# A scan, eight routed experts and a Fourier mixer on one core: turned second layers, sorted last experts, 128-row blocks with stationary rows, and new orders

## The chip, the cores and the metric

The kernel runs on one core of a Trainium2 chip. The metric is the device time of one execution in microseconds. Three executions of the kernel before gave 446.72, 448.24 and 451.06 us; the median is 448.24.

## What is computed

Three networks follow one another: a chunked linear-attention scan, a mixture of eight experts in which the gate of a token can keep the expert of the token before, and a Fourier mixer with a two-layer network.

```python
# scan over a sequence of 768, for 4 batches and 8 heads
M = np.einsum('bhin,bhjn->bhij', Cc, Bc) * L          # L: decay between i and j, causal
y = M @ xc + (Cc @ state) * decay_to_i
state = decay_full * state + sum_j(Bc * xc * decay_from_j)
# experts: 3072 tokens of 256, 8 experts of 256 x 1024 x 256
e = fresh_e if s == 0 or local_gate < 0.5 else prev_e
out[b, s] = p[e] * (np.maximum(x[b, s] @ w1[e], 0.0) @ w2[e])
# mixer
u = x + np.real(np.fft.fft(np.fft.fft(x, axis=1), axis=2))
un = (u - mean) / sqrt(var + 1e-6)
return u + np.maximum(un @ w_ch1, 0.0) @ w_ch2
```

## The kernel before

Each value of the two-layer networks is split in a high and a low part, and a product is three matmuls: high by high, high by low, low by high. All instructions stand in an order that the program text fixes; each engine takes its own in that order, and SyncE (SP) takes the loads in order too.

*Scan* (`phase_a`). Twelve rounds (six chunks of 128 tokens, two pairs of batches) run `scores`, `mask`, `intra`, `keep`, `carry`, `rows`; `state_mm` multiplies the state's update. `routing` finds expert and rank of a chunk's tokens in small VectorE steps that a queue spreads over the rounds (`gap`, `place`), and `leave` scatters the rows, by the addresses `si`, into `xs_buf`, sorted by expert. When the last chunk but one has left, `xe`, the first 256 rows of expert 0, is loaded.

*Experts* (`ffn`, `moe_expert`). The first 256 rows of expert 0 (`EARLY`) go first, then its rest, then the seven others by size, with the capacities `CAPS`. In the first layer a 128 x 128 block of w1 is stationary and the expert's n rows move (`mm1`); ScalarE writes the relu `hh`, VectorE the low part `hl`. In the second layer a 128-row tile of `hh` or `hl` is stationary and 256 columns of w2 move, 24 matmuls for each tile, however many rows it has (`mm2`). `evac` scales a tile and GpSimd (POOL) scatters it into `y_tok` by token. Meanwhile the next expert's weights are loaded (`load_w`) and split (`high` on ScalarE, `low` on VectorE) and its rows transposed (`split_x`). `prep_wch` converts the mixer's weights in eight chunks. Behind the experts stands a branch on overfull experts (`overflow`, line 936), which isn't taken here.

*Mixer*. `load_z` and `load_k` read `y_tok` back by batch, `fold` reduces 768 points to six products of 128, `stage_a`, `correct` and `stage_b` are the transforms as matmuls, `residual` adds rows and mix, `center_` subtracts the mean. `group` runs the two-layer network for 512 rows at a time, six times; a batch has six tiles of 128 rows. `keep_clock` issues matmuls whose result isn't used, and so does `warm` in the scan.

Of the kernel before, what the change touches and what calls it, by code (L numbers as in the profile page):

```python
# [7 lines left out]
FP32 = mybir.dt.float32  # L8
# [12 lines left out]
CAPS = (128, 480, 448, 416, 416, 384, 352, 320)  # L21
# [5 lines left out]
CP, CT = 128, 129  # L27

# [8 lines left out]
WARM = 10  # L37
CA = {}
_o = 0
for _n, _w in (  # L40
    ("pm", 2), ("cmask", 128), ("w1", 9), ("ident", 128), ("w0", 9), ("tri", 128), ("ones", 128),
    ("tbl", 8), ("tid", 24), ("rid", 4), ("sel", 128), ("dlt", 12), ("cap", 8),
):
    CA[_n] = (_o, _w)
    _o += _w
# [5 lines left out]
def tile_kernel(ctx: ExitStack, tc: tile.TileContext, io):  # L51
# [9 lines left out]
    wst = ExitStack()  # L61
    wraw = wst.enter_context(tc.tile_pool(name="wraw", bufs=2))
    wsp = wst.enter_context(tc.tile_pool(name="wsp", bufs=2))
# [25 lines left out]
    y_tok = dram.tile([NTOK, D], FP32, name="y_tok")  # L89
    groups = set()  # L90
# [15 lines left out]
    def prep_wch(i, pool):  # L106
        n = 512
# [8 lines left out]
        else:  # L116
# [8 lines left out]
            dst = [t.rearrange("p k d -> p (k d)") for t in dst]  # L125
        hw, lw = raw[:, :, 1], raw[:, :, 0]
        v = pool.tile([128, n], I32, tag="cv", name="cv")
        e = pool.tile([128, n], I32, tag="ce_", name="ce_")
        r = pool.tile([128, n], FP32, tag="cr", name="cr")
# [6 lines left out]
        vf = v.bitcast(FP32)  # L136
        A.activation(out=dst[0], in_=vf, func=ACTF.Copy)
        ef = e.bitcast(FP32)
        G.tensor_tensor(out=ef, in0=vf, in1=dst[0], op=ALU.subtract)
        G.tensor_tensor(out=dst[1], in0=ef, in1=r, op=ALU.add)  # L140
# [5 lines left out]
    def expert(j):  # L146

        if j not in regs:
            regs[j] = nc.values_load(
                who[0:1, j:j + 1], engines=(mybir.EngineType.SP,), min_val=0, max_val=NE - 1 if j else EARLY,  # L150
                skip_runtime_bounds_check_because="a permutation of 1..7; a minimum with 256",
            )
        return regs[j]

    def load_w(e, part=None, static=False):

        i = bass.ds(e if static or e == 0 else expert(e), 1)
        if part != 1:
            r1 = wraw.tile([128, 2, F], FP32, tag="raw", name="r1")
            SP.dma_start(out=r1, in_=io["w1"][i].rearrange("o (k p) f -> p (o k) f", p=128))  # L160
            raws[e, 0] = r1
        if part != 0:
            r2 = wraw.tile([128, 8, D], FP32, tag="raw", name="r2")
            SP.dma_start(out=r2, in_=io["w2"][i].rearrange("o (k p) d -> p (o k) d", p=128))
            raws[e, 1] = r2

        def pieces():
            out = []
            for k, n, sh in ((0, "w1", [128, 2, F]), (1, "w2", [128, 8, D])):
                r = raws.pop((e, k))  # L170
                hi = wsp.tile(sh, FP32R, tag=n + "h", name=n + "h")
                lo = wsp.tile(sh, FP32R, tag=n + "l", name=n + "l")
# [16 lines left out]
                for q in range(2):  # L189
                    if not (ahead and k):  # L190
                        high(q)
                    if ahead:
# [13 lines left out]
    def keep_clock(pool, n):  # L206

        wps = pool.tile([128, 512], FP32, tag="mm1", name="wps")
        for _ in range(n):
            PE.matmul(out=wps, lhsT=fa[:, 0, :], rhs=fa[:, 0:4, :].rearrange("p n k -> p (n k)"), start=True, stop=True)  # L210
# [7 lines left out]
    def phase_a():  # L218
        with ExitStack() as st:
# [15 lines left out]
            def load(c, names=("ct", "bt", "x", "bn")):  # L235
# [8 lines left out]
            rp, dps = mb[:, 0:256], mb[:, 256:384].rearrange("p (u d) -> p u d", u=2)  # L244
# [3 lines left out]
                wsp.tile(sh, FP32R, tag=n, name="scr")  # L248
# [118 lines left out]
            st2 = [big.tile([128, 2, 64], FP32, name=f"st{q}") for q in range(2)]  # L367
# [84 lines left out]
            def state_mm(i):  # L452

                c, bp = pairs[i]
                for u in range(2):
                    for q in range(4):
# [966 lines left out]
```

## Time and profile before

| | |
|---|---|
| time of three executions | 446.72, 448.24, 451.06 us |
| the profiled execution | 449.59 us |
| its span, first to last instruction | 447.8 us |
| TensorE busy with matmuls | 420.5 us, 94% |
| VectorE, ScalarE, GpSimd busy | 270.1, 182.3, 147.6 us |
| mean granted TensorE clock | 0.981 |

The profile is of one execution. A matmul's end is modelled and matmuls overlap, so that a busy TensorE is not yet one at its peak, and busy time holds the matmuls that only keep the clock. The time is 1.8 us longer than the span. A granted clock of 1.00 is 2.4 GHz, 0.50 is 1.2 GHz.

### The profile page before, as it was taken

The page shows a single profiled execution, that of the slowest core. Times are in us where ns is not written, and L with a number is a line of the kernel's source. Part 1 is how long each engine was busy: PE and PEld are TensorE (multiplying, and loading weights), DVE is VectorE, ACT ScalarE, POOL GpSimd, SP SyncE. Part 2 cuts the span into 40 slices and gives each one's busy share as a digit, 9 for nine tenths or more (in the row PEclk, how much of TensorE's full clock was granted, in tenths as well). Part 3 has the DMA queues.
Part 4 walks back from the last instruction along what each step waited for, and adds up shares of the span by engine and source line. Part 5 has one row for each costly group of instructions (what it writes and reads, how often), then busy time and mean ns, then how long its engine had stood idle before and what let it go on. Part 6 is the DMA issues. An engine that isn't in the chain of part 4 may idle for free.

```text
span 447.8 us, 8833 instructions
## 1 busy us (share of the span) xinstructions
PE 420.5 (94%) x3403; PEld 366.3 (82%) x3403; DVE 270.1 (60%) x717; ACT 182.3 (41%) x399; POOL 147.6 (33%) x191
## 2 busy tenths in 40 slices
PE   8798788899999999999989979999999999999997
PEld 4476666479999999999989937679899998998986
DVE  3668889864583747566576408857537586654341
ACT  2255455334555454555454312343413433332230
POOL 1264876531006162433405530818003431400000
PEclk9899999999799999999999969999999999999999
DMA  8799711227356363736463037001402010010101
GB/s 287 228 309 310 284 50 52 73 84 264 111 183 209 117 213 126 247 99 211 153 199 109 34 101 250 23 2 47 143 25 94 1 35 14 14 35 11 38 1 47
DMA packets 32650, 54.10 MB, mean 121 GB/s; under 512 B 3161, under 2 KB 21882, under 8 KB 32601
## 3 DMA queue, kind: packets, MB, share of 16 engines
q1 hardware_dynamic: 29272, 45.73, 31.2%
q0 software_dynamic: 2816, 7.45, 4.8%
q8 instruction: 28, 0.46, 0.4%
q10 hardware_dynamic: 512, 0.28, 0.2%
q14 instruction: 22, 0.17, 0.1%
HBM read 41.50 MB, written 12.08 MB: 120 GB/s over the span
## 4 chain that ended last, share of the span: by engine, by line
PE 76%; DMA 8%; DVE 6%; ACT 5%; issue 2%; POOL 2%; SPq 0%; POOLq 0%; ACTq 0%; DVEq 0%
PE mm L857 30%; PE mm L844 26%; DMA y_tok<-y,ids 5%; PE tl L495 3%; PE tp L871 3%; PE g L411 2%; PE mb L259 2%; PE f L1125 2%; DMA xk<-y_tok,rix 2%; DVE mt L419 1%; PE yb L442 1%; DMA xn<-xs_buf 1%; ACT x1t L449 1%; PE cps L1139 1%; PE yb L431 1%
## 5 line engine op out<-in xcount | busy, mean ns | idle before, releaser
L849 DVE SCALAR_TENSOR_TENSOR hl<-mm,hh 128x512 fp32r<-128x512 f32 (+8 forms) x120 | 68.9, 589 | 49.8 <-ACT hh L848 49.6
L848 ACT ACTIVATE hh<-mm 128x512 fp32r<-128x512 f32 (+8 forms) x120 | 61.6, 518 | 78.7 <-PE mm L844 78.4
L909 POOL DMA_INDIRECT y_tok<-y,ids x26 | 32.5, 1249 | 94.6 <-ACT y L908 75.0
L857 PE MATMUL mm<-w2h,hh 128*128 128x256 f32 (+3 forms) x224 | 63.4, 283 | 0.0
L857 PE MATMUL mm<-w2l,hh 128*128 128x256 f32 (+3 forms) x224 | 62.6, 280 | 0.0
L857 PE MATMUL mm<-w2h,hl 128*128 128x256 f32 (+3 forms) x224 | 62.6, 279 | 0.0
L857 PE MATMUL mm<-c2h,hh 128*128 128x256 f32 x192 | 54.5, 284 | 0.0
L857 PE MATMUL mm<-c2l,hh 128*128 128x256 f32 x192 | 53.8, 280 | 0.0
L857 PE MATMUL mm<-c2h,hl 128*128 128x256 f32 x192 | 53.8, 280 | 0.0
L844 PE MATMUL mm<-xh,w1h 128*128 128x416 f32 (+7 forms) x144 | 48.2, 340 | 2.9 <-DVE hl L849 2.4
L844 PE MATMUL mm<-xh,w1l 128*128 128x416 f32 (+7 forms) x144 | 47.4, 334 | 0.0
L857 PEld LDWEIGHTS mm<-w2l,hh 128*128 128x128 f32 (+3 forms) x224 | 40.1, 179 | 0.1
L857 PEld LDWEIGHTS mm<-w2h,hh 128*128 128x128 f32 (+3 forms) x224 | 40.1, 179 | 0.1
L857 PEld LDWEIGHTS mm<-w2h,hl 128*128 128x128 f32 (+3 forms) x224 | 40.0, 179 | 0.1
L844 PE MATMUL mm<-xh,c1h 128*128 128x512 f32 x96 | 39.5, 411 | 0.6 <-ACT xh L873 0.6
L183 DVE TENSOR_TENSOR w2l<-r,w2h 128x1024 fp32r<-128x1024 f32 (+1 forms) x18 | 22.0, 1228 | 27.1 <-ACT w2h L180 27.1
L844 PE MATMUL mm<-xh,c1l 128*128 128x512 f32 x96 | 37.9, 395 | 0.0
L844 PE MATMUL mm<-xl,w1h 128*128 128x416 f32 (+7 forms) x144 | 36.7, 336 | 0.0
L857 PEld LDWEIGHTS mm<-c2l,hh 128*128 128x128 f32 x192 | 36.2, 188 | 0.1
L857 PEld LDWEIGHTS mm<-c2h,hh 128*128 128x128 f32 x192 | 36.1, 188 | 0.1
L857 PEld LDWEIGHTS mm<-c2h,hl 128*128 128x128 f32 x192 | 36.1, 188 | 0.0
L419 DVE TENSOR_TENSOR mt<-g,ca 128x512 f32<-128x512 f32 x48 | 31.3, 676 | 6.7 <-PE g L411 6.6
(329 smaller groups left out, 840.2 us busy)
## 6 DMA issues: line engine op xcount, KB each, us to landing
r<-in_w_dram SPq DMA_DIRECT2D x16, 1024.0 KB, 9.1
rawc<-in_wc_dram SPq DMA_DIRECT2D x8, 512.0 KB
out_dram<-o SPq DMA_DIRECT2D x24, 128.0 KB, 1.7
z<-y_tok SPq DMA_DIRECT2D x3, 768.0 KB
xs_buf<-scr SPq DMA_DIRECT2D x8, 265.0 KB, 8.5
xn<-xs_buf SPq DMA_DIRECT2D x4, 530.0 KB, 6.5
c1h<-in_x_dram SPq DMA_DIRECT2D x4, 512.0 KB, 5.2
xk<-y_tok SPq DMA_DIRECT2D x4, 512.0 KB, 3.7
```

What stands on the lines that cost most here:

```text
L183: V.tensor_tensor(out=l_[:, x:y], in0=r_[:, x:y], in1=h[:, x:y], op=ALU.subtract)
L259: PE.matmul(out=ps[:, 0:w], lhsT=wrm[:, 0:128], rhs=wrm[:, 0:w], start=True, stop=True)
L411: PE.matmul(out=gp[q][:, u].rearrange("p h i -> p (h i)"), lhsT=lds[c]["bt"][r:r + 32, 2 * bp + u, :], rhs=ch[r:r + 32, u].rearrange("p q ...
L419: V.tensor_tensor(out=m[:, :, 2 * q:2 * q + 2, :], in0=gp[q], in1=cc("cmask").unsqueeze(1).unsqueeze(1).to_broadcast([128, 2, 2, 128]), op ...
L495: PE.matmul(out=tl[:, 128 * g:128 * g + 137], lhsT=x1t[:, g, u, :], rhs=ca[:, o:o + 137], start=(g == 0), stop=(g == 1), skip_group_check= ...
L844: PE.matmul(out=ps[:, 0:n], lhsT=w[:, d, f * 128:(f + 1) * 128], rhs=x[:, d, 0:n], start=(k == 0), stop=(k == 5))
L848: A.activation(out=hf, in_=ps[:, 0:n], func=ACTF.Relu)
L849: V.scalar_tensor_tensor(out=hl[:, f, 0:n], in0=ps[:, 0:n], scalar=0.0, in1=hf, op0=ALU.max, op1=ALU.subtract)
L857: PE.matmul(out=ps[0:m, :], lhsT=h[:, f, t * 128:t * 128 + m], rhs=w[:, f, :], start=(k == 0), stop=(k == 23))
L871: PE.transpose(ps[d][:, t * 128:(t + 1) * 128], src(t, d), ident)
L909: w = G.indirect_dma_start(out=y_tok, out_offset=bass.IndirectOffsetOnAxis(ap=ids[0:m, t:t + 1], axis=0), in_=y[0:m, :], in_offset=None, b ...
L1125: PE.matmul(out=ps[:, k2, :], lhsT=r[:, zi, :], rhs=fa[:, ci, :], start=(i == 0), stop=(i == len(terms) - 1),)
```

## The change

It joins several edits.

- *Turned second layers.* For experts with n rows, n not a multiple of 128 and at most 480, the second layer has a 128 x 128 block of w2 stationary and n columns of `hh` or `hl` moving, twice 24 matmuls. The result is the transpose of what is wanted: ScalarE copies it (`yt`), and TensorE transposes it back under the next expert's first layer (`flush`).
- *Blocks of 128 rows.* Where n is 128, the rows are stationary and w1 moves, 512 columns at a time: 12 matmuls in place of 48. Eight transposes bring the relu back.
- *Sorted last experts.* `PLACE` sets a new order of sizes, with two experts of 416 rows last. Their rows are sorted by token into `xs_part` (`sort_rows`). Expert 6 then computes its first 288 rows, in which lie those of batches 0 and 1; expert 7 its first 128, with those of batch 0, and then its other 288; and at last expert 6 its other 128. Batch 0's transform is issued between these pieces (`rest`, `turn`), in tiles that free weight buffers lend (`homes`).
- *Orders.* At the scan's end `leave` and the addresses come ahead of the last chunk's steps; the last chunk's ranks in expert 0 begin behind row 256, so that its scatters don't wait for `xe`. Loads of weights in the scan stand behind a GpSimd `memset` (`held`). Rows are loaded two experts ahead. Batch 1's fold is all on VectorE; batches 2 and 3 have one correction together (`nyquist`). The branch on overflow comes at the end, and recomputes the mixer.
- *Scan.* `carry` and `state_mm` work on halves of the array in place of quarters.
- `keep_clock` is no longer called, and `warm` at the scan's end three times, not four.

```diff
-CAPS = (128, 480, 448, 416, 416, 384, 352, 320)
+CAPS = (128, 480, 448, 384, 352, 320, 416, 416)
+PLACE = (7, 6, 3, 2, 1, 5, 4)
+SORTED = (NE - 2, NE - 1)
+LEAD = {NE - 2: (2 * S, 288), NE - 1: (S, 128)}
...
@@ carry
-                        for q in range(4):
-                            r, o = 32 * q, 64 * (q % 2)
+                        for g in range(2):
+                            r = 64 * g
                             PE.matmul(
-                                out=yb[o:o + 64, q // 2, 128 * u:128 * u + 128], lhsT=s_st[bp][r:r + 32, u, :],
-                                rhs=ops[i][0][r:r + 32, u, :], start=(u == 0), stop=False, skip_group_check=True,
+                                out=yb[:, g, 128 * u:128 * u + 128], lhsT=s_st[bp][r:r + 64, u, :],
+                                rhs=ops[i][0][r:r + 64, u, :], start=(u == 0), stop=False, skip_group_check=True,
                             )
...
@@ the rounds of the scan
-                if i in (5, 7):
-                    ws = load_w(0, i // 7)
+                if i in (6, 8):
+                    g = load_w(0, i // 8, late=True)
+                    ws = g if i == 6 else ws
...
-                    leave(0)
-                    leave(0)
+                    gap(3, True)
+                    while scq:
+                        leave(0)
...
@@ ffn
+        flip = n % 128 and n <= 480
...
+        if n == 128:
+            for f in range(4):
+                hook(f)
...
+            for q in range(2):
+                ps = ps1.tile([128, CAP], FP32, tag="mm1", name="mm1")
+                for k, (w, x, d) in enumerate(terms):
+                    PE.matmul(
+                        out=ps, lhsT=x[:, d, 0:n], rhs=w[:, d, q * 512:q * 512 + 512], start=(k == 0), stop=(k == 5)
+                    )
...
+            flush()
+            for q in range(2):
+                ps = pst.tile([128, CAP], FP32, tag="tp", name="tp")
+                for f in range(4):
+                    PE.transpose(ps[:, 128 * f:128 * f + 128], hr[:, 4 * q + f, :], ident)
...
+        if flip:
+            yt = back_of(e)
+            yt = [yt[:, d, 0:n] for d in range(2)]
+            for d in range(2):
+                ps = ps2.tile([128, CAP], FP32, tag="mm2", name="mm2")
+                for k, (f, h, w) in enumerate(order2):
+                    PE.matmul(
+                        out=ps[:, 0:n], lhsT=w[:, f, 128 * d:128 * d + 128], rhs=h[:, f, 0:n], start=(k == 0),
+                        stop=(k == 23),
+                    )
+                    if k == 11:
+                        hook(8 + 2 * d)
+                A.activation(out=yt[d], in_=ps[:, 0:n], func=ACTF.Copy)
+                hook(9 + 2 * d)
...
@@ experts
+                at = AT.get(e, (2, 3, 4, 5, 8, 8))
+                for _ in range(at.count(i) if more else 0):
+                    next(ws, None)
...
+                if more and (e, i) == (e, MORE.get(e, 9)):
+                    next(ws, None)
+                    ws = load_w(e + 2) if e + 2 < NE else None
...
@@ transform
+        moe_expert(pools, last, *cur, lambda i: next(late) if i == 4 else None, n=n7)
+        homes_z()
+        load_z(0)
+        moe_expert(pools, last, *cur, rest, n=CAPS[last] - n7, t0=1)
+        wt.pop(last)
+        homes(1, wide(last))
+        moe_expert(pools, last - 1, *most, turn, n=CAPS[last - 1] - n6, t0=3)
...
+    with tc.manual_schedule():
+        lead, nr = experts()
+        transform(lead)
+    with tc.If(nr > 1):
+        overflow(pools, nr)
+        transform(None)
```

The order on VectorE near the scan's end, where the last chunk but one gets its addresses `si` and the last chunk starts its routing (`mx`, `kd`, `ls`), before and then after:

```order
L508 TENSOR_REDUCE mx<-scr 128x2
L512 TENSOR_SCALAR kd<-scr 128x2
L515 TENSOR_TENSOR ls<-scr,mx 128x16
L521 SCALAR_TENSOR_TENSOR cand<-ls,cb 128x16
L524 TENSOR_REDUCE ff<-cand 128x2
L526 SCALAR_TENSOR_TENSOR kd<-kd,ff 128x2
L183 TENSOR_TENSOR w1l<-r_696,w1h 128x512
L603 TENSOR_REDUCE rk<-ro 128x4
L607 SCALAR_TENSOR_TENSOR si<-f__1270,rk 128x4
```

```order
L639 SCALAR_TENSOR_TENSOR si<-f__1197,rk 128x4
L660 TENSOR_SCALAR nfirst<-mb 128x1
L539 TENSOR_REDUCE mx<-scr 128x2
L543 TENSOR_SCALAR kd<-scr 128x2
L546 TENSOR_TENSOR ls<-scr,mx 128x16
L552 SCALAR_TENSOR_TENSOR cand<-ls,cb 128x16
L555 TENSOR_REDUCE ff<-cand 128x2
L557 SCALAR_TENSOR_TENSOR kd<-kd,ff 128x2
L212 TENSOR_TENSOR w1l<-r_767,w1h 128x512
```

The addresses stood behind seven instructions of the next chunk, and now stand ahead of them.

The order on TensorE around batch 0's transform (`f`: the second product, `cps`: the correction, `mix`: the second stage), before and then after:

```order
L1125 MATMUL f<-fa,r_5440 128x128 x6
L1139 MATMUL cps<-w,fa 128x1 x6
L1155 MATMUL mix<-fb,pt 128x129
L1156 MATMUL mix<-fb,pt 128x128
...
L1155 MATMUL mix<-fb,pt 128x129
L1156 MATMUL mix<-fb,pt 128x128
L210 MATMUL wps<-fa 128x512 x5
L871 MATMUL tp<-ca,n 128x128 x8
L844 MATMUL mm_5609<-xh,c1h 128x512
```

```order
L1451 MATMUL mix<-fb,pt 128x129
L1452 MATMUL mix<-fb,home 128x128
L965 MATMUL tp<-ca,yt 128x128 x4
L965 MATMUL tp<-ca,yt 32x128 x2
L910 MATMUL mm_3417<-w1h,xh 128x512
L910 MATMUL mm_3417<-w1l,xh 128x512
...
L910 MATMUL mm_3425<-w1h,xl 128x512 x2
L922 MATMUL tp<-ca,hr 128x128 x8
```

Between the mix and the first matmuls of the mixer's network (`c1h`) stood clock keeping; now expert 7's transposes back (`yt`) and expert 6's last block stand there, and the transposes of `n` come in the middle of that block's second layer.

The order on TensorE in expert 0's rest, 128 rows, first layer, before (one of eight column blocks) and then after (one of two):

```order
L844 MATMUL mm_1707<-xh,w1h 128x128
L844 MATMUL mm_1707<-xh,w1l 128x128
L844 MATMUL mm_1707<-xh,w1h 128x128
L844 MATMUL mm_1707<-xh,w1l 128x128
L844 MATMUL mm_1707<-xl,w1h 128x128 x2
```

```order
L910 MATMUL mm_1647<-w1h,xh 128x512
L910 MATMUL mm_1647<-w1l,xh 128x512
L910 MATMUL mm_1647<-w1h,xh 128x512
L910 MATMUL mm_1647<-w1l,xh 128x512
L910 MATMUL mm_1647<-w1h,xl 128x512 x2
L922 MATMUL tp<-ca,hr 128x128 x8
```

The operands have changed sides: the weights moved past are 512 columns wide, and the relu's eight transposes follow.

## Rows read from the trace of the kernel before

**Rows 1.** Table of stages: span, each engine's busy us (instructions), granted clock, DMA.

```profile
93.30:118.40 25.10, 24.20 (x178) 23.96 (x179) 13.49 (x43) 10.55 (x26) 5.06 (x6) 0.86 0.54 186
118.40:258.00 139.60, 136.82 (x980) 131.71 (x979) 86.45 (x136) 71.56 (x126) 52.22 (x41) 1.00 0.47 154
258.00:286.20 28.20, 23.77 (x93) 13.90 (x92) 16.23 (x57) 7.67 (x19) 9.14 (x17) 0.88 0.42 139
```

**Rows 2.** Chain that ended last, experts: start us, us, engine, tile, line.

```profile
105.33 1.30 PE mm L844 x12
...
118.61 10.40 PE mm L844 x48
129.01 0.88 PE tp L871 x8
129.88 11.28 PE mm L857 x96
...
184.18 9.24 PE mm L844 x48
```

**Rows 3.** The table of stages, two microseconds in expert 0.

```profile
110.00:112.00 2.00, 2.00 (x12) 2.00 (x11) 1.35 (x2) 0.28 (x2) 0.00 (x0) 0.50 0.04 12
```

**Rows 4.** Timeline between experts and mixer, by engine: idle before in brackets.

```profile
258.84 0.91 POOL L909 DMA_INDIRECT y_tok<-y,ids  x1 [0.59 <-ACT y L908]
...
264.49 1.43 SPq L1040 DMA_DIRECT2D z<-y_tok  x3
...
267.88 0.56 DVE L1070 TENSOR_TENSOR eo<-z 128x384 f32<-128x384 f32 x1 [14.79 <-DMA z<-y_tok]
...
261.07 11.75 PE L210 MATMUL wps<-fa 128*128 128x512 f32 x20 [3.06 <-ACTq L936]
...
274.96 1.79 PE L1125 MATMUL f<-fa,r 128*128 128x128 f32 x12 [0.79 <-DVE r L1086]
...
279.74 4.46 PE L210 MATMUL wps<-fa 128*128 128x512 f32 x10
284.03 1.15 PE L871 MATMUL tp<-ca,n 128*128 128x128 f32 x8
```

**Rows 5.** Timeline at the scan's end, by engine.

```profile
79.60 0.16 DVE L508 TENSOR_REDUCE mx<-scr 128x2 f32<-128x16 f32 x1
...
81.31 0.16 DVE L607 SCALAR_TENSOR_TENSOR si<-f__1270,rk 128x4 int32<-128x4 f32 x1
...
88.88 0.38 SPq L620 DMA_DIRECT2D xe<-xs_buf  x1
...
92.35 0.60 PE L871 MATMUL tp<-ca,xe 128*128 128x128 f32 x4
```

**Rows 6.** Timeline, SP and ScalarE: issue and first use of expert 7's w1.

```profile
218.96 0.37 SPq L160 DMA_DIRECT2D r<-in_w_dram  x1
...
224.88 1.06 ACT L180 ACTIVATE w1h<-r 128x1024 fp32r<-128x1024 f32 x1
```

**Rows 7.** The table of DMA issues: KB each, median us from issue to landing.

```profile
r<-in_w_dram SPq DMA_DIRECT2D x16, 1024.0 KB, 9.1
...
y_tok<-y,ids POOLq DMA_INDIRECT x26, 3.2
```

**Rows 8.** Chain that ended last, mixer's network.

```profile
316.84 11.19 PE mm L844 x48
...
379.04 1.23 PE cps L1139 x12
```

**Rows 9.** Instructions of the branch, line 936: ns, first start us.

```profile
L936 PEldq COMPARE_BRANCH  x1: 3662/3662/3662, 255.8 to 255.8; - x1
```

**Rows 10.** Timeline and chain of one round of the scan, TensorE.

```profile
52.63 0.41 PE L457 MATMUL mb<-xt,c2l 128*32 128x64 f32 x16
53.66 0.73 PE L495 MATMUL tl<-ca,x1t 128*128 128x137 f32 x4 [0.62 <-ACT x1t L449]
...
47.75 0.60 PE yb L431 x16
```

More of the change, by code (lines that the diff above doesn't have):

```diff
@@ L35 @@
 GATE = -1.5 * 2.0 ** -23
-WARM = 10
 CA = {}
@@ L582, in routing @@
                 )
+                if c + 2 == NC:
+                    PE.matmul(out=rp[:, 8:9], lhsT=cc("ones"), rhs=ac[:, 0:1, nb], start=True, stop=True)
                 exo = sm.tile([128, nb, NE], FP32, tag="exo", name="exo")
@@ L861, in ffn @@
+        for t in range(0 if flip else tiles):
+            ps = ps2.tile([128, CAP], FP32, tag="mm2", name="mm2")[:, 0:D]
+            m = min(128, n - 128 * t)
+            for k, (f, h, w) in enumerate(order2):
+                PE.matmul(
+                    out=ps[0:m, :], lhsT=h[:, f, t * 128:t * 128 + m], rhs=w[:, f, :], start=(k == 0), stop=(k == 23)
+                )
+                if n == 128 and k == 11:
+                    hook(12)
             evac(t, ps[0:m, :], m)
             hook(8 + t)
+    turns = [0]
@@ new lines, in transform @@
+        if lead is None:
+            homes_z()
+            for i in range(1, 3):
+                homes(i, wide(i))
+            for b in range(NB):
+                load_z(b)
+                load_k(b)
+                all_of(b)
+                for g in {1: (0, 1, 2), 3: (3, 4, 5)}.get(b, ()):
+                    group(g, lambda i: None, split_n(g))
+            return
+        most, cur, late = lead
+        last = NE - 1
+        n6, n7 = (LEAD[e][1] for e in SORTED)
+        nxt = None
@@ new lines, in rest @@
+        def rest(i):
+            if i == 0:
+                next(late)
+            if i == 10:
+                stage_a(0, 0)
+            if i == 7:
+                near = xp.tile([128, 4, D], FP32, tag=f"xl{NE % 2}", name="near", bufs=1)
+                two = sm.tile([128, 2 * D], I32, tag="cv", name="near").bitcast(FP32)
+                home["pt0"] = sm.tile([128, 4 * 128], I32, tag="cv", name="pt").bitcast(FP32)
+                home["pt0"] = home["pt0"].rearrange("p (a b) -> p a b", a=4)
+                home["near"] = near, [two[:, D * k:D * k + D] for k in range(2)]
+                load_k(0)
+                run(0, 0, 3)
+                run(0, 1, 3)
@@ new lines, in transform, with hook @@
+        for g in range(6):
+            cur = nxt
+            def hook(i):
+                nonlocal nxt
+                if (g, i) in ((1, 3), (1, 4), (1, 5)):
+                    next(nyq)
+                if (g, i) in ((0, 3), (1, 1), (2, 1)):
+                    load_k(g + 1)
+                if (g, i) == (0, 7):
+                    center(0, 4, 6, (A,))
+                if i == 10 and g < 5:
+                    nxt = split_n(g + 1)
+                for p in plan.get((g, i), ()):
+                    run(*p)
+                if (g, i) == (0, 7):
+                    scale(0)
+            group(g, hook, cur)
```

752 lines of the change are left out of this document (486 added, 266 removed), and 6 rows, old and new, of the table plan.

## Prediction

> **What bounds the kernel now.** Read first the table of stages [rows 1]: from 118.4 us on TensorE has a matmul in flight for 136.8 of 139.6 us, so there only fewer or cheaper matmuls help. Two stretches are different. From 93.3 to 118.4 us its clock averages 0.86, and from 258.0 to 286.2 us, between the last expert's last matmul and the first matmul of the last network, it is busy for 23.8 of 28.2 us, but with what? The timeline there [rows 4] answers: 20 rows of clock-keeping matmuls, and a chain of other units. The last scatter of expert rows starts at 258.84, the load of z that waits for it at 264.49, VectorE begins on z at 267.88 after an idle of 14.79 us, TensorE starts the second part of the first transform at 274.96 and transposes the result at 284.03. The 28.2 us are one latency chain, during which nothing of the experts is left to compute. So I ask of each part of the change whether it cuts matmul time, or puts work under that chain.
>
> **Prices of a matmul.** First layer: 48 matmuls take 10.40 us at 480 columns, 9.24 at 416 [rows 2] and 11.19 at 512 [rows 8], that is 217, 192.5 and 233 ns each, or 0.423 ns a column plus 16.6 ns. Second layer before: 96 of 256 columns in 11.28 us, 117.5 ns each [rows 2]. A turned one has n columns; with the same slope from that anchor it costs 212 ns at 480, 199 at 448, 158 at 352, 145 at 320 and 131 at 288. A 128-column matmul takes 108 ns (1.30 us for 12), a transpose 110 ns (0.88 us for 8) [rows 2].
>
> **The change part by part.**
>
> *Scan.* The carry goes from 8 matmuls on quarters of the array to 4 on halves, the state's product likewise with twice the columns. Today the carry takes 0.60 us for 16 passes of 128 columns, and the rows product 0.73 us for 4 passes of 137 on the whole array [rows 10]: 0.29 ns a column on a quarter, 1.33 on the whole. Half way, some 0.55, the carry costs 8 x 128 x 0.55 = 0.56 us, a gain of 0.04 a pair. The state's product goes from 0.41 us to about 0.56, but TensorE then stands idle for 0.62 us for the copy x1t anyway [rows 10], so that covers it; uncovered it is +0.15 x 10 = 1.5 us. I take 0, bounds -1 to +2 (the products are also twice as wide on VectorE and GpSimd). The Trainium skill, TensorE: Matmul & The Clock Gate, Part 3 (packing small matmuls), speaks against this edit: concurrency comes from many small tiles in distinct row and column groups. By that rule the carry gains nothing and the state's product doubles; the trace's cheap quarter passes agree with it, and the sum would be +2 instead of 0.
>
> *Scan's end.* The experts begin when xe lands: load at 88.88, transposes at 92.35 [rows 5]. That load waits for scatters whose addresses si come at 81.31, behind seven VectorE instructions of the next chunk that start at 79.60. The order in the section on the change shows si moved ahead of them, to about 80.0: **-1.3 us**, and the four scatters and the load follow. The warm-up matmuls that vanish stood in TensorE's wait for xe; removing them gains nothing. The last chunk's scatters no longer wait for xe, which only helps later loads.
>
> *Expert 0.* From 105.33 to the 480-row expert at 118.61 are 13.3 us [rows 2]. In it TensorE falls to the lower of its two levels, 1.2 GHz: granted 0.50 at 110 to 112 us [rows 3], after a run of 128-column matmuls; the average of 0.86 over 25.1 us [rows 1] makes that 7 us at half speed, so 3.5 us lost. Now: 12 matmuls of 512 columns 2.80, 8 transposes back 0.88, 8 for the next expert 0.88, second layer 24 x 117.5 ns = 2.82, and 0.6 us waiting for the relu between: 8.0 us. **-5.3 us**, if the clock holds; at 1.2 GHz for the last 5 us it is -2.8.
>
> *Experts 1 to 7, matmuls.* Second layers turned: 480 10.2, 448 9.5, 352 7.6 and 320 6.9 us, instead of 11.28, 11.28, 8.46 and 8.46: -5.3. The two 416s become 288 turned (6.3) and 128 (2.8) instead of 11.28: -2.2 each, -4.4. Turned outputs must be transposed back, 40 times 0.11: +4.4. First layers of the split ones: 288 columns 6.6 and a block of 128 rows 2.8 + 0.9 instead of 9.24: +1.1 each, +2.2. More transposes of inputs +0.4, waits for the relu in two blocks +1.2. Sum -1.5. The same stretch has 2.8 us without a matmul now; the turned outputs add two ScalarE copies an expert, and VectorE (86 of 139.6 us busy, [rows 1]) stays below TensorE. Giving 1.5 us for that, the stretch comes to **0**; bounds -2.5 and +4. The sorting adds some 30 small VectorE instructions and 8 scatters to engines with room, and its loads are issued two experts ahead.
>
> *Between experts and the last network*, now 28.2 us. Batch 0's rows are complete after the lead of expert 7. From there: copy and start of the scatter 0.8 us; start of scatter to load issue 5.65 us today [rows 4] (the median landing of a scatter is 3.2 [rows 7], so 3.7 to 5.7); load issue to VectorE's start 3.4; VectorE to the second product 7.1 (267.88 to 274.96): 15 to 17 us. TensorE has under it the rest of expert 7 (6.6 + 6.3) and the first product (1.5): 14.4, leaving a wait of 0.5 to 2.6; I take 1.5. From the second product to the transposes the chain is 9.07 us; TensorE has second product, correction and mix (274.96 to 279.74, 4.7), expert 7's transposes back (0.7), expert 6's block (2.8, 0.9, 0.6 of wait, half of 2.8): 11 us, so no wait. The block's other half covers the split of the transposed rows. What stays of the 28.2 us: both products, correction and mix 1.5 + 4.7 = 6.2, transposes 0.9, wait 1.5, 0.2 of slack = 8.8. **-19.4 us.** The clock keeping goes, and so does TensorE's 3.06 us of idle at the branch [rows 4].
>
> *Group 0 of the last network*: 30.6 us now (286.2 to 316.84 [rows 8]). Batch 1's second fold moves from GpSimd to VectorE (two parts took VectorE 6.8 us for batch 0, so +3.4), and batch 1's z is loaded only after expert 7's last scatters, which stand behind five row additions on GpSimd: by the delays above some 6 us after the group's start, where VectorE waits in order ahead of the subtractions that free TensorE's buffers. Its matmuls sum to 11.19 + 11.28 + 0.88 + 6.2 = 29.6, so 1.0 us of waits is in it now. I take 1.7 of waits for 1.0: **+0.7**, bounds -1 and +3.
>
> *Nyquist column.* One correction for two batches: **-1.2 us** (12 rows in 1.23 us [rows 8]); its small operations lie on GpSimd under group 1.
>
> *The branch* on the overflow moves to the end. TensorE's compare took 3.66 us [rows 9]. On SyncE it now follows the last output store, whose landing covers part of it: **+1.5**, bounds 0 and 3.7. The Trainium skill, Runtime: NRT & Kernel Launch, section on instruction fetch mechanics, says that a taken branch out of the current code window has its target fetched before execution goes on; the 3.66 us agree, and by it alone the term is +3.7.
>
> **Sum:** -1.3 - 5.3 + 0 - 19.4 + 0.7 - 1.2 + 1.5 = -25.0. From the profiled 449.59 us (span 447.8) this gives 424.6. That execution lies 1.35 above the median, so against the median of 448.24 I predict **423 us**.
>
> **Rivals.** (1) *Weights come late.* A load of 1 MB of w1 is issued at 218.96 and used at 224.88 without more wait [rows 6], so 5.9 us suffice there; the one landing that the page shows is 9.1 us [rows 7]. The stages of 320 and 288 rows leave, from the conversion that frees the buffer half way through a second layer to the use after three first-layer groups, only some 5.4 us. ScalarE would then wait in order and hold up the relus. For five experts, 1.6 us each that the three buffers don't absorb: +8, 431 us. Against it: before, the first conversion came after two groups, sooner than now.
> (2) *The cover tears.* If z of batch 0 waits for more than the one scatter (the load waits for every scatter in the queue, and chunks of weight conversion stand on GpSimd before it), each us over 17 is a TensorE wait, and after 3 us of idle the clock falls as behind 258.0: the average of 0.88 over 28.2 us [rows 1] is 6.8 us at half speed, 3.4 us lost. With 6.6 us of wait: +10, 433 us.
> (3) *Slower than before.* Late weights as in (1), but at the 9.1 us of the page: 3.7 us a load for seven experts, and each such idle also lowers the clock as it does behind 258.0, 3.4 us: 7 x 7.1 = 50, 473 us. It decides from 3.6 us lost per expert (25 / 7). Today's 5.9 us without wait speaks against it.
> (4) *The cover works better*: landing in 3.7 us, no stall in group 0, no cost of the branch: -7, 416 us.
>
> **How the numbers follow.** Forecast 0.5, (4) 0.2, (1) 0.14, (2) 0.1, (3) 0.03, the remaining 0.03 no effect because several terms cancel. The forecast's own terms leave 415 to 431; with (4) below and (1) and (2) above, the range is 411 to 435. A run of this kernel shows no difference below about 1%. Faster by over 1%: 0.94; within: 0.03; slower: 0.03.
>
> **What would show it.** Right: 12 matmuls of 512 columns for expert 0 at granted clock 1.00 and the 480-row expert starting near 112 us; between the end of the first layer of expert 7's rest and group 0's first matmul no TensorE gap above 3 us; group 0 starting near 259 us; the span ending 2 to 4 us after the last output store. Wrong: ScalarE's conversions of w1 waiting for a DMA, a clock below 1.00 behind expert 7, VectorE waiting for z under group 0's first layer for more than 4 us.

## The result, and the profile after

| | before | after |
|---|---|---|
| times | 446.72 to 451.06 us | 425.28, 421.84, 420.60, 420.29 us |
| median | 449.61 us (four runs) | 421.22 us |
| profiled execution, span | 449.59, 447.8 us | 425.28, 423.2 us |
| TensorE busy with matmuls | 420.5 us | 404.0 us |

The ratio is 0.940, with a 95% interval of 0.933 to 0.947: 27 us off. The profiled execution is the longest of those shown. A fifth, timed beside them, took 423.16 us. In the five, the time falls as the mean granted clock rises: 425.28 (0.980), 423.16 (0.984), 421.84 (0.992), 420.60 (0.996), 420.29 (0.998).

First the page of the kernel after, busy times and then the granted clock in 40 slices.

```profile
span 423.2 us, 8212 instructions
...
PE 404.0 (95%) x3063; PEld 353.6 (84%) x3063; DVE 281.3 (66%) x772; ACT 188.5 (45%) x411; POOL 144.9 (34%) x204
...
PEclk9899999868999999999999999999999999999999
```

The table of stages of the same execution, columns as in [rows 1]: the scan's end, expert 0's first 256 rows, its 128-row rest, experts 1 to 7 with batch 0's transform, and groups 0 and 3.

```profile
80.00:92.40 12.40, 11.45 (x65) 6.59 (x65) 8.30 (x46) 3.93 (x13) 4.97 (x7) 0.59 0.27 87
...
95.70:108.90 13.20, 13.18 (x99) 13.18 (x99) 6.67 (x28) 4.13 (x12) 2.94 (x3) 0.87 0.55 182
108.90:117.10 8.20, 7.83 (x55) 6.76 (x54) 4.96 (x9) 6.97 (x11) 0.98 (x1) 1.00 0.57 198
117.10:263.70 146.60, 144.74 (x936) 135.67 (x935) 109.63 (x241) 82.61 (x161) 55.71 (x57) 1.00 0.55 176
263.70:293.50 29.80, 29.63 (x207) 26.90 (x205) 21.43 (x66) 10.61 (x25) 7.43 (x13) 1.00 0.39 125
...
345.60:373.10 27.50, 27.50 (x195) 25.54 (x194) 18.93 (x63) 11.21 (x27) 6.98 (x16) 1.00 0.07 21
```

Experts 1 to 7 and the transform, which took 139.6 + 28.2 us in two stages [rows 1], are one stage of 146.6 us at full clock, and TensorE stands idle for 1.9 us of it. Group 0 begins at 263.7 us. Behind the first 20 us the clock falls only at the scan's end, to 1.2 GHz from 82 to 92 us and again around 97 us. In the kernel before the same table reads 1.00 from 76 to 100 us.

How the gap closed stands in the chain that ended last, after:

```profile
236.12 6.32 PE mm L932 x48
242.44 4.81 PE mm L950 x36
247.26 1.34 PE f L1393 x12
248.59 1.59 PE mm L950 x12
250.19 1.66 PE f L1393 x12
251.84 1.23 PE cps L1434 x12
...
260.81 0.60 DVE hl L926
261.45 0.99 PE tp L993 x7
```

The first product of batch 0 (`f`) runs inside expert 7's second layer, the second right behind it; between the correction and the transposes (`tp`) TensorE has expert 6's block, and it waits for nothing longer than 0.25 us.

### The profile page after: what moved, and what is told of

Read it like the earlier page. It is cut to its first block, busy times and chain, and to the rows that moved or that the text cites. A ratio compares the mean times of both kernels' runs of the same rounds, so it can differ in the third digit from the quotient of the medians.

```text
span 423.2 us, 8212 instructions
## 1 busy us (share of the span) xinstructions
PE 404.0 (95%) x3063; PEld 353.6 (84%) x3063; DVE 281.3 (66%) x772; ACT 188.5 (45%) x411; POOL 144.9 (34%) x204
## 4 chain that ended last, share of the span: by engine, by line
PE 79%; DVE 10%; ACT 5%; DMA 2%; issue 2%; POOL 0%; DVEq 0%; ACTq 0%
PE mm L932 27%; PE mm L974 18%; PE mm L950 11%; PE tl L524 3%; PE tp L993 3%; PE f L1393 2%; PE g L440 2%; PE mb L288 2%; DVE mt L448 2%; PE yb L471 1%; PE g L288 1%; PE mm L910 1%; DMA r<-in_w_dram 1%; ACT x1t L478 1%; DVE hl L939 1%
## 5 line engine op out<-in xcount | busy, mean ns | idle before, releaser
L939 DVE SCALAR_TENSOR_TENSOR hl<-mm,hh 128x512 fp32r<-128x512 f32 (+7 forms) x112 | 65.9, 593 | 46.2 <-ACT hh L938 45.8
L938 ACT ACTIVATE hh<-mm 128x512 fp32r<-128x512 f32 (+7 forms) x112 | 57.3, 521 | 67.3 <-PE mm L932 67.3
L932 PE MATMUL mm<-xh,w1h 128*128 128x288 f32 (+6 forms) x128 | 42.7, 340 | 1.5 <-DVE hl L939 1.0
L932 PE MATMUL mm<-xh,w1l 128*128 128x288 f32 (+6 forms) x128 | 41.3, 329 | 0.0
L950 PE MATMUL mm<-hh,w2h 128*128 128x288 f32 (+4 forms) x96 | 32.2, 335 | 0.0
L950 PE MATMUL mm<-hh,w2l 128*128 128x288 f32 (+4 forms) x96 | 31.6, 329 | 0.0
L932 PE MATMUL mm<-xl,w1h 128*128 128x288 f32 (+6 forms) x128 | 31.5, 328 | 0.0
L950 PE MATMUL mm<-hl,w2h 128*128 128x288 f32 (+4 forms) x96 | 31.5, 328 | 0.0
L932 PE MATMUL mm<-xl,c1h 128*128 128x512 f32 x96 | 29.9, 392 | 0.0
L932 PEld LDWEIGHTS mm<-xh,w1h 128*128 128x128 f32 x128 | 24.7, 193 | 4.2 <-DVE hl L939 2.6
```

The lines of the kernel that those rows point to most:

```text
L932: PE.matmul(out=ps[:, 0:n], lhsT=w[:, d, f * 128:(f + 1) * 128], rhs=x[:, d, 0:n], start=(k == 0), stop=(k == 5))
L938: A.activation(out=hf, in_=ps[:, 0:n], func=ACTF.Relu)
L939: V.scalar_tensor_tensor(out=hl[:, f, 0:n], in0=ps[:, 0:n], scalar=0.0, in1=hf, op0=ALU.max, op1=ALU.subtract)
L950: PE.matmul(out=ps[:, 0:n], lhsT=w[:, f, 128 * d:128 * d + 128], rhs=h[:, f, 0:n], start=(k == 0), stop=(k == 23),)
```

## The experiments

All were timed beside the kernel before, five rounds each but for e6 and e7 with three. The kernel before had medians of 446.55, 448.38 and 448.35 us beside e1 to e4, e5 to e8 and e9 to e12, so that ratios are compared; 0.01 is 4.5 us. The experiments overlap (e3's last block stands under the transform that e6 takes away), so that their effects don't add up to the 27 us. Not undone by themselves are the new places of the scatters and addresses, `held`, the loads two experts ahead and batch 1's fold.

| run | change to the kernel after | median, us | ratio, 95% interval |
|---|---|---|---|
| e1 | none | 420.51 | 0.941, 0.937 to 0.945 |
| e2 | second layers not turned | 423.89 | 0.950, 0.945 to 0.955 |
| e3 | 128-row blocks, w1 stationary | 438.54 | 0.981, 0.977 to 0.985 |
| e4 | scan on quarters | 422.32 | 0.946, 0.941 to 0.950 |
| e5 | no branch | 419.85 | 0.936, 0.931 to 0.940 |
| e6 | transform behind both experts | 443.94 | 0.990, 0.986 to 0.993 |
| e7 | block not under the transform | 429.42 | 0.957, 0.952 to 0.962 |
| e8 | count first | 420.62 | 0.939, 0.933 to 0.945 |
| e9 | e8, loads sooner | 419.93 | 0.938, 0.935 to 0.941 |
| e10 | e9, scan on quarters | 419.68 | 0.939, 0.935 to 0.943 |
| e11 | e10, three more matmuls | 417.75 | 0.933, 0.930 to 0.936 |
| e12 | a correction for each batch | 421.43 | 0.942, 0.937 to 0.946 |

**The same kernel (e1).** 

> The changed kernel once more, unchanged, as the base for the others. Theory A (the profiled execution was an unlucky one: its granted clock lay at 0.50 from 82 to 92 us and from 96 to 99 us, which the shorter times beside it did not have): the median comes to 420 to 422 us, and a profile with a mean granted clock of 0.99 or more has xe's transposes (line 993) start near 92 us instead of 94.68 and the span end near 418.5. Theory B (the late start of the experts is there in every execution): xe's transposes start at 94 us or later at full clock too.

The median bears out A's range, but the profile can't decide: it is again of the longest execution (424.63 us, clock 0.978), with the same fall at 82 to 92 us. The other six executions had a mean clock of 0.995 or 0.996. Half speed from 82 to 92 us alone costs 0.012 of such a mean, so they hardly had that fall. What a scan without it does can be read in e6 below, whose scan is that of the kernel after and whose clock held until the transposes of `xe`. In its timeline and its table of stages:

```profile
75.13 0.73 PE L524 MATMUL tl<-ca,x1t 128*128 128x137 f32 x4 [0.47 <-ACT x1t L478]
...
86.89 0.38 SPq L654 DMA_DIRECT2D xe<-xs_buf  x1
...
90.22 0.66 PE L993 MATMUL tp<-ca,xe 128*128 128x128 f32 x4 [1.21 <-DVE cnt L844]
```

```profile
80.00:90.30 10.30, 7.18 (x35) 3.85 (x35) 8.14 (x43) 3.45 (x12) 6.06 (x7) 1.00 0.24 79
```

The transposes start at 90.22 us, and B falls. The stretch from the scan's 21st rows product (`tl`) to them was 16.7 us before. With the scan of after it is 15.1 us at full clock (e6), 16.6 and 16.7 where the clock averages 0.72 from 80 to 92.4 us (e2, e7), and 17.8 where it averages 0.59 to 0.61 (after, e1, e3, e5, e12). So at full clock the change shortens it by 1.6 us, and the fall of the clock takes up to 2.7.

**Second layers not turned (e2).**

```diff
-        flip = n % 128 and n <= 480
+        flip = False
```

> The changed kernel with the turned second layers undone: every second layer multiplies 128-row tiles by 256 columns again, also those of the sorted experts' 288 rows. Theory A (turned layers are a small gain, since the transposes back eat most of it): 480 rows 11.3 for 11.4 us, 448 11.3 for 10.7, 352 8.5 for 8.3, 320 8.5 for 7.8, and 288 rows twice 8.5 for 7.1, so +4 us in all, 425 us. Theory B (nothing, since the second layers' time lies under loads and conversions of the next weights, which set the pace of the experts): within 1 us. Theory C (turned layers also shorten the chain to the scatter of batch 0, because their copies come late): below the base by 1 us or more.

0.009 of ratio, 4.1 us: A, though the intervals just touch. The chain of e2, 480 and 448 rows:

```profile
124.97 5.66 PE mm L974 x48
...
130.98 5.73 PE mm L974 x48
...
147.27 8.40 PE mm L974 x72
...
156.02 2.88 PE mm L974 x24
```

And the kernel after:

```profile
128.52 5.28 PE mm L950 x24
134.13 5.38 PE mm L950 x24
...
151.01 7.36 PE mm L950 x36
158.71 2.55 PE mm L950 x12
```

For 480 rows turning saves 11.39 - 10.66 = 0.7 us, and the eight transposes back take 0.9 (0.44 us for four in the same chain): nothing is gained. For 448 it is 11.28 - 9.91 = 1.4 us, for 0.9 us of transposes. By these rows the gain is larger where the last 128-row tile is not full; 480 fills most of it.

**The 128-row blocks with w1 stationary again (e3).** The branch `n == 128` of the first layer gives way to the loop over eight column blocks.

> The changed kernel with the three blocks of 128 rows (expert 0's rest, expert 7's first rows, expert 6's last) back to w1 stationary: 48 matmuls of 128 columns instead of 12 of 512 and eight transposes back. Theory A (what the blocks give is the clock: 128-column runs let TensorE fall to 1.2 GHz, as at 110 to 117 us of the kernel before): the granted clock reads 0.50 for some 7 us in at least expert 0's rest, +3 us for each block that falls, 424 to 431 us. Theory B (the clock holds, the cost is that of the matmuls alone): 48 x 71 ns = 3.4 us against 2.8 + 1.3 us with the transposes, so each block is 0.5 to 0.7 us shorter, 419 us.

17.9 us, more than either theory had. The table of stages of e3 over the three blocks: expert 0's rest, expert 7's first rows, expert 6's last.

```profile
108.90:122.50 13.60, 12.46 (x82) 12.32 (x81) 6.53 (x16) 7.30 (x15) 0.98 (x1) 0.75 0.34 110
232.60:241.50 8.90, 8.90 (x80) 8.71 (x79) 4.42 (x13) 4.24 (x13) 5.41 (x5) 1.00 0.21 76
261.00:279.30 18.30, 14.15 (x84) 14.01 (x82) 8.92 (x32) 4.41 (x14) 6.22 (x12) 0.72 0.19 59
```

With the rows stationary the first takes 8.2 us (table above), and the other two, after:

```profile
227.90:236.00 8.10, 7.67 (x53) 6.60 (x52) 5.00 (x10) 4.69 (x10) 5.19 (x5) 1.00 0.23 85
255.40:263.70 8.30, 7.99 (x55) 6.87 (x53) 7.94 (x26) 4.60 (x10) 6.20 (x12) 1.00 0.10 35
```

So 5.4, 0.8 and 10.0 us, 16.2 in all. In the middle block the clock holds, and 48 matmuls of 128 columns cost 112 ns each on average, not B's 71 (the chain has 1.29, 1.29 and 2.81 us for 12, 12 and 24; the prediction's own price was 108): 5.4 us, against 2.8 + 1.3. In the other two the clock falls, as A says, but not by the 128 columns alone, since the middle block holds 1.00 with the same 48. In both TensorE had stood idle shortly before, waiting for VectorE, as TensorE's timeline of e3 shows:

```profile
112.13 0.33 PE L931 MATMUL mm<-xh,w1h 128*128 128x128 f32 x1 [1.14 <-DVE hl L938]
...
266.66 0.47 PE L931 MATMUL mm<-xh,w1h 128*128 128x128 f32 x1 [4.15 <-DVE hl L938]
```

Idle time alone doesn't do it either: in e8 below TensorE waits 1.39 us in expert 0's rest and the clock stays at 1.00. What makes the clock fall stays open.

In the last block each of eight column blocks needs VectorE's `hl` to free its accumulator, and VectorE is in batch 0's statistics then. With the rows stationary the block's first twelve matmuls and its relu need VectorE not once; `hl` comes behind the transposes. That is a part of the cover which neither theory had. Of the block's 10.0 us it is some 4, the clock at 0.50 from 266.7 to 276.7 us some 5, and the price of the matmuls the rest (an estimate from these rows).

**The scan on quarters (e4).** `carry` and `state_mm` as in the kernel before.

> The changed kernel with the scan's carry and state product back on quarters of the array (state products 64 columns wide again on VectorE, GpSimd and ScalarE). Theory A (the halves cost time, at the steps on VectorE behind the wider state: each round of the scan came 0.05 to 0.3 us later, 1.2 us by line 524's last rounds, 75.67 to 76.87 us): those rounds come back to 75.7 us, -1.2 us, 420 us. Theory B (the halves cost nothing, and the lag comes from weights loaded and converted at other places): the last rounds stay at 76.8 us, and the time stays within 0.5 us. Theory C (the halves gain, 0.04 us a pair and a shorter wait for x1t): slower by 0.5 us or more.

In the rounds A is right: from the first rows product to the 21st (`tl`) the timelines read 19.82 to 75.67 us before (55.85), 19.69 to 76.87 after (57.18), 17.65 to 73.67 in e4 (56.02). The last of these in the timelines of after and of e4:

```profile
76.87 0.73 PE L524 MATMUL tl<-ca,x1t 128*128 128x137 f32 x4 [0.46 <-ACT x1t L478]
```

```profile
73.67 0.50 PE L524 MATMUL tl<-ca,x1t 128*128 128x137 f32 x2 [0.47 <-ACT x1t L478]
```

What the wider state costs shows in its tile `sn`, after:

```profile
L494 DVE TENSOR_TENSOR sn<-mb,ca x10: 401/415/425, 13.8 to 67.2; 128x256 f32<-128x256 f32 x10
L503 POOL TENSOR_TENSOR sn<-st,sn x8: 719/726/765, 25.8 to 71.0; 128x256 f32<-128x256 f32 x8
```

The three numbers are the shortest, the median and the longest in ns. Before, the medians were 281 and 456 ns, and on ScalarE 338 where it is now 391. That these steps make the lag, and not TensorE's own, is argued from these rows and not tried apart. Yet the whole got no shorter (0.946, not to be told from 0.941): in e4's six executions the mean clock was 0.977 to 0.991, in six of e1's seven 0.995 or 0.996. The 1.2 us are real, and something behind them takes them back; e8 to e11 look for it. In e4's profile a lower clock fits: it is 0.83 from 80 to 92.4 us, and from the 21st rows product to the transposes of `xe` (73.67 to 89.77) it takes 16.1 us, where e6 takes 15.1. The Trainium skill, TensorE: Matmul & The Clock Gate, Part 3 (packing small matmuls), which lets small tiles in distinct row and column groups run at the same time, was right in direction: state product 0.41 to 0.66 us, carry 0.60 to 0.65 for half the matmuls.

**No branch (e5).** The `If` at the end, its overflow and its recomputation are left out.

> The changed kernel without the branch on overfull experts at its end (and without the recomputation behind it, which these inputs never take). Theory A (the branch at the end costs what the tail grew by: from the last output tile's addition to the end of the span 2.8 us before, 4.0 us after): -1.2 us, 419.3 us, and the span ends some 2.8 us after the last addition. Theory B (the whole 3.66 us of the compare stand in the time): -3.7 us, 416.8 us. Theory C (it lies under the landing of the last stores): within 0.5 us.

The ratios (0.936 and 0.941) can't be told apart by their intervals; the tail can be read. The last additions of the kernel after and of e5:

```profile
418.68 0.48 DVE L1533 SCALAR_TENSOR_TENSOR o<-mm,ve,home 128x256 f32<-128x256 f32 x1 [2.31 <-PE mm L974]
```

```profile
span 421.6 us, 8190 instructions
...
418.44 0.48 DVE L1533 SCALAR_TENSOR_TENSOR o<-mm,ve,home 128x256 f32<-128x256 f32 x1 [2.31 <-PE mm L974]
```

From the addition's end to the span's end: 423.2 - 419.16 = 4.0 us with the branch, 421.6 - 418.92 = 2.7 without. A: 1.3 us. TensorE's compare at the branch is still there in the kernel after, as the instructions of line 1670 show (ns, start in us):

```profile
L1670 PEldq COMPARE_BRANCH  x1: 3378/3378/3378, 416.4 to 416.4; - x1
```

It takes 3.38 us, but begins while TensorE's last matmuls run (they end at 418.6) and ends at 419.8, 0.6 us behind the last addition. So only 0.6 us of it stand in the tail, and SyncE's own compare takes 50 ns. What the 1.3 us consist of is not shown.

**The transform behind both experts (e6), and the block alone taken from under it (e7).**

```diff
 # e7
-        moe_expert(pools, last - 1, *most, turn, ...)
+        moe_expert(pools, last - 1, *most, lambda i: None, ...)
+        turn(0)
+        turn(12)
 # e6: both of expert 7's and expert 6's pieces first, then
+        load_z(0); rest(7); rest(10); turn(0); turn(12)
```

> The changed kernel with batch 0's transform issued behind both experts, not between their pieces: first expert 7's other 288 rows and expert 6's last 128, then the loads of batch 0, the folds, both products, correction, mix, residual and the transposes. Theory A (the cover is the largest part of the gain): the chain from the scatter to the network stands open again, 0.8 + 5.7 + 3.4 + 7.1 + 9.1 + 1.7 us less the 8 us of TensorE's own work in it, and a fall of the clock in it: +17 to +22 us, 438 to 443 us. Theory B (the gain came from sorting and sizes, so that z of batch 0 is long there and only the residual's chain is open): +8 to +12 us.

> The changed kernel with only expert 6's last block of 128 rows taken out from under batch 0's transform: the block comes first, then the second product, correction, mix, residual and transposes. Theory A (the block's 7.2 us cover 7 of the 10.9 us between second product and transposes, the rest is TensorE's own mix): +6 to +7 us, and 3 us more if the clock falls in the idle time, 427 to 431 us. Theory B (VectorE and GpSimd set that stretch, whether TensorE has the block or not, since the block's relu waits for VectorE too): +2 us or less.

Both A. e6 is 0.049 of ratio above e1, 21.7 us; its TensorE timeline has the old gap again:

```profile
263.86 2.90 PE L1393 MATMUL f<-fa,home 128*128 128x128 f32 x12 [10.23 <-DVE home L1349]
```

and the table of stages from expert 6's last second layer to group 0, at a clock of 0.64:

```profile
250.50:282.80 32.30, 16.92 (x84) 15.33 (x84) 15.64 (x53) 4.74 (x16) 10.80 (x18) 0.64 0.46 156
```

e7 is 0.016 above e1, 7 us. Of the cover, then, the block gives a third; that the rest lies under expert 7's other rows is a subtraction and wasn't tried apart.

**The count first (e8), and the loads sooner (e9).**

```diff
 # e8
-            while low[0] < 4:
-                next(ws)
-                low[0] += 1
-            cps = pg.tile([128, 2, 2, 128], FP32, tag="g0", name="cps")[:, 0, 0, 0:NE]
+            cps = yb[:, 1, 0:NE]
             (count as before)
+            while low[0] < 4:
+                next(ws)
+                low[0] += 1
 # e9, in the hooks of expert 0's first 256 rows
-            if i < 6:
+            for _ in range((2, 1, 1, 1, 1)[i] if i < 5 else 0):
                 next(od)
-            if i == 2:
+            if i == 0:
                 xn = load_x(pools, 0)
-                xn1 = load_x(pools, 1)
+            if i == 1:
                 ws = load_w(1)
+                xn1 = load_x(pools, 1)
```

> The changed kernel with the scan's last count (cnt, line 844) written to another bank of the accumulators and read on VectorE ahead of the last conversions of w2. The work is the same. Theory A (at the scan's end the order gained 1.3 us for the addresses, but TensorE's transposes of xe now wait for the count, 1.1 to 1.2 us of idle in each profile, and no longer for the rows): -0.7 to -1.2 us, xe's transposes wait for the load, 3.5 us behind its issue. Theory B (the rows land no sooner than the count): within 0.3 us.

> As e8, with the sort of the experts by size (order) two column blocks sooner and the loads in another order: expert 0's rest is asked for at the first block, expert 1's weights at the second and ahead of its rows, where both stood at the third, behind the rows. Theory A (what the scan's end gains is given back in expert 0's rest: there ScalarE waits 2.07 us for expert 1's w1, 7.5 us after its issue, and TensorE 1.4 + 0.5 us for the relu): the issue moves from 98.2 to 95 or 96 us, the wait goes, -1.5 to -1.9 us in executions at full clock, 418.5 to 419.5 us. Theory B (the landing is set by the load's own bandwidth or by the buffers' release, not by its issue): within 0.5 us.

Of after, the timeline at the scan's end:

```profile
81.17 0.16 DVE L639 SCALAR_TENSOR_TENSOR si<-f__1197,rk 128x4 int32<-128x4 f32 x1
...
88.62 0.38 SPq L654 DMA_DIRECT2D xe<-xs_buf  x1
...
94.46 0.16 DVE L844 TENSOR_SCALAR cnt<-cps 128x8 f32<-128x8 f32 x1
...
94.68 0.66 PE L993 MATMUL tp<-ca,xe 128*128 128x128 f32 x4 [1.13 <-DVE cnt L844]
```

The transposes begin 6.1 us behind the issue of the load, 3.5 before [rows 5], and what releases them is the count. Most of that is the low clock: at full clock, in e6, the count releases them too, but 3.3 us behind the issue. In e8 the wait is 0.68 us and still the count's, 2.8 us behind the issue: some 0.5 us gained there. The total shows no difference. The profile of e8, at a clock of 1.00 throughout, tells why a sooner start gains little:

```profile
98.24 0.75 SPq L187 DMA_DIRECT2D r<-in_w_dram  x1
...
105.71 1.06 ACT L209 ACTIVATE w1h<-r 128x1024 fp32r<-128x1024 f32 x1 [2.07 <-DMA r<-in_w_dram]
...
107.31 0.33 PE L922 MATMUL tp<-ca,hr 128*128 128x128 f32 x1 [1.39 <-ACT hr L915]
```

Expert 1's w1 lands 7.5 us behind its issue, ScalarE waits for it in order, and with it the relu `hr` and TensorE: expert 0's rest takes 9.7 us (102.96 to 112.68), not 8.2. In the profile of after the experts started 4.8 us later and ScalarE waited only 0.38 us there; in e2, e6 and e7, with the scan and the loads of after, 1.97, 0.75 and 2.48 us. Of the 4.8 us, 1.7 lie ahead of the first rows product, where the clock from 10 to 20 us was 0.83 and in e8 1.00, and 3.3 at the scan's end. In e9 the issue comes at 98.92 us, 7.9 us behind the transposes of `xe` in place of 8.3: less than A had, since it still stands behind the load of expert 0's rest in SyncE's queue, and that load waits until 97.3 us for the last chunk's scatters. It lands within 6.0 us, ScalarE waits no more, and the rest takes 8.4 us (104.36 to 112.77); in e10, the same loads at full clock, 8.2 (100.66 to 108.83). The ratio is that of e8 all the same: the wait went as A says, a gain in the time isn't shown.

**Quarters too (e10), and more matmuls (e11).** e11 adds `warm(1, 256)` three times in the scan's last two rounds, in TensorE's waits.

> As e9, with the scan's carry and state product on quarters. Theory A (with the two waits behind it gone, the 1.2 us that quarters save in the scan's rounds reach the end): -1 us against e9, 417.5 to 418.5 us. Theory B (the wait for the loads, or a clock that falls more often with the thinner scan, takes it back, as the longer time of e4 beside shorter rounds says): no less than e9, and a granted clock below 0.99 in its runs.

> As e10, with three matmuls of 256 columns whose result isn't used in TensorE's waits of the scan's last two rounds. Theory A (the clock falls at 80 to 92 us because TensorE's work there is thin, and a little more keeps it up): no stretch at 0.50 between 76 and 100 us in the profile, mean clock 0.99 and more in all runs, 1 to 3 us below e10. Theory B (the fall doesn't hang on so little work): the same falls, and up to 1 us slower than e10.

e10 fits B: no less than e9, clocks from 0.983 to 0.999. Its two executions at 0.999, 417.30 and 418.16 us, lie at or just below where A had them. e11 fits A, six executions of 416.56 to 419.12 us with clocks of 0.996 to 1.000, but doesn't show it: its interval overlaps e10's, and four of e10's six had 0.995 or more without the added matmuls. Nor does its table of stages over the scan's end, which has 1.00 where e1 has 0.72, since e10's own profile reads 1.00 there too. For e11:

```profile
76.00:100.00 24.00, 21.84 (x171) 17.21 (x172) 16.10 (x82) 8.98 (x27) 10.60 (x12) 1.00 0.37 122
```

In e10 and e11 the transposes of `xe` wait for the load of `xe` at last (0.77 and 0.73 us), no longer for the count. e11 is the shortest version found: 0.933 against 0.941 for e1, their intervals just apart, some 3 us; against the kernel before, 30 us.

**A correction for each batch (e12).** 

> The changed kernel with one correction for each of batches 2 and 3 again, in place of the one for both. Theory A (the term of the sum): +1.2 us, in group 3, which takes 27.5 us now and 28.7 then. Theory B (TensorE waits in group 3 for VectorE, which now has fewer small steps, and the 1.7 us by which group 3 is shorter come from there): +1.7 us.

The total is the same within its interval, so that no gain in the time is shown; the chain of e12 has group 3 from 341.79 to 370.65, 28.9 us, where after it is 27.5: 1.4 us, closer to A, which had 1.2.

## Why the prediction was right, point by point

The time (423 us predicted, 421.2 measured) and the places of the two large gains, expert 0's rest and the gap, were right. By stages, against the profiled execution after:

| term | predicted | measured | |
|---|---|---|---|
| scan | 0 (-1 to +2) | +1.3 | 57.18 for 55.85 us |
| scan's end | -1.3 | +1.0 | transposes of `xe` 2.3 us later, less the scan's 1.3; at full clock -1.6 (e6) |
| first 256 rows | 0 | +1.2 | 13.2 for 12.0 us, granted clock 0.87; in e8, at 1.00, 12.0 |
| expert 0's rest | -5.3 | -5.1 | 8.2 for 13.3 us; in e8 9.7 |
| experts 1 to 7 and gap | 0 and -19.4 | -21.2 | 146.6 for 167.8 us |
| group 0 | +0.7 | -0.8 | 29.8 for 30.6 us |
| Nyquist column | -1.2 | -1.7 | group 3, 27.5 for 29.2 us |
| branch | +1.5 | +1.2 | the tail 4.0 for 2.8 us |

The rows sum to -24.1 us (the spans to -24.6), where the forecast had -25.0. That they meet so closely is luck in part: four terms came out dearer, by 5.0 us together, and four cheaper, by 4.1. The 480-row expert starts at 117.06 us in this profile, at 113.02 in e6 and 112.68 in e8, where the clock held longer ("near 112 us" was forecast). Those 4.0 to 4.4 us off 425.28 give 420.9 to 421.3 us, an estimate; the executions at a mean clock of 0.992 to 0.998 took 420.29 to 421.84.

*Scan.* The step "that covers it" was half right: the wait for `x1t` did shrink (0.26 us where it was 0.62 [rows 10]), but the same wider state takes 0.13 us more on VectorE and 0.27 on GpSimd, where the rounds' routing steps queue. The 1.2 to 1.3 us were only in the bounds.

*Scan's end.* The order was right: the addresses come 5.6 us behind the 21st rows product before (75.67 to 81.31 [rows 5]), 4.3 after, the predicted 1.3, and the load follows them by 7.5 us as it did (7.6). At full clock the transposes of `xe` gain 1.6 us (e6). What the step left out are two things: in the profile of after the clock averages 0.59 from 80 to 92.4 us, which takes 2.7 us, and the count of the last chunk's routing ends some 0.5 us later than the rows land (e8).

*Expert 0's rest* came out by its own terms: 2.8 + 1.3 + 1.1 + 2.9 us. Its reason was the clock, and e3 shows the clock and, beside it, the 112 ns of a 128-column matmul. But the clock doesn't fall by "a run of 128-column matmuls" as such: e3's middle block is one and holds 1.00, and before, TensorE had just waited for VectorE:

```profile
109.50 0.33 PE L844 MATMUL mm<-xh,w1h 128*128 128x128 f32 x1 [0.87 <-DVE hl L849]
```

*Experts and gap.* The cover held, with next to nothing to spare. The timelines after have the scatter, the load, and VectorE's first and last step of the folds and last of the subtractions:

```profile
236.91 0.97 POOL L1089 DMA_INDIRECT y_tok<-y,ids  x1 [0.70 <-ACT y L1088]
...
239.38 0.90 SPq L1299 DMA_DIRECT2D home<-y_tok  x2
...
243.30 1.02 DVE L1333 TENSOR_TENSOR xn<-home 128x384 f32<-128x384 f32 x2
...
250.33 0.28 DVE L1352 SCALAR_TENSOR_TENSOR home<-home 128x128 f32<-128x128 f32 x1
...
260.22 0.59 DVE L1511 TENSOR_SCALAR home<-home,mv 128x256 f32<-128x256 f32 x1
```

From the start of the scatter to the issue of the load it is 2.5 us, where 3.7 to 5.7 were taken, so that the wait of 1.5 us in the sum isn't there. But VectorE takes up z only when expert 7's `hl` is done, 3.9 us behind the issue. It ends the folds at 250.6 us, when the second product has just begun (250.15), and the subtractions at 260.8, 0.3 us before the transposes. The chain from the second product to the transposes, 9.1 us in the prediction, takes 11.0. e6 measures the cover at 21.7 us. What the prediction didn't see is that the block under the transform would itself have waited for VectorE, had its rows not been stationary: 4.15 us in e3, with the clock at 0.50 behind it.

*Turned layers* gave some 4 us in e2. By the working's prices that edit is worth 5.3 us for four experts and twice 8.46 - 6.3 = 4.3 for the 288 rows, less 4.4 for the transposes back: 5.2. For 480 rows they give nothing: 10.66 us, where 10.2 were taken.

*Group 0.* The step "1.7 of waits for 1.0" was mis-sized: TensorE waits 0.2 us in it. VectorE doesn't wait for z there.

*Branch.* The size was right. But the prediction carried TensorE's 3.66 us over to SyncE, whose compare takes 50 ns; TensorE's own, 3.38 us, lies for the most part under its last matmuls and the last addition (e5).

*Rivals.* (1), late weights, showed in one place of after, where ScalarE waits 0.79 us at 185.17 for w1 and TensorE 0.7, not 8 us; and where the experts start sooner, at expert 1's w1 (e2, e6, e7, e8). (2) and (3) didn't show: the clock reads 1.00 from 100 us to the end. (4) came closest: no stall in group 0, the landing short; but the branch costs its 1.2 us, and the scan's 1.3 were in no rival.

## What to carry to other kernels

A long chain between two stages is covered by work that doesn't use the chain's engines: taking the block out from under it cost 7 us (e7), and leaving it there in a form that needs VectorE, which had the chain, cost 10 (e3, the fall of the clock with it). When an address, a load or a store is moved ahead, follow the release to the instruction that starts next, and look for the second wait that ends just behind the first: here the count, then the next expert's weights. And where a stage's times scatter, read the granted clock of that stage before explaining the time, and look for a trace with the same code at another clock: the new order at the scan's end loses 1.1 us in one and gains 1.6 in another.

## What was not expected of the hardware

One and the same scan met a different clock at its end from trace to trace: an average of 0.59 from 80 to 92.4 us in after, 0.72 in e2, 0.98 in e6. In the five executions of after the time went with the mean clock, 425.28 us at 0.980 and 420.29 at 0.998. The mean clock isn't all: e8 took 421.42 us at 1.000 and 419.01 at 0.996. In e10 the six executions spread from 417.30 (0.999) to 422.55 us (0.986), with three more short matmuls (e11) from 416.56 to 419.12; that the matmuls did it isn't shown.

At full clock 128 columns took 112 ns on average in 48 matmuls (e3), so that a 512-column matmul (234 ns in the block of 12 that takes 2.81 us) moves four times the columns in little over twice the time.
